# Layer-1 wo products moved into the tail of the forward attention, and shorter chains of small operations, in a two-layer decode kernel with backward pass

## The chip, the cores and the metric

The kernel runs on one core of a Trainium2 chip. The metric is the device time of one execution in microseconds (us); the time before is the median of three runs.

## The reference, cut to what matters

Two layers share one set of weights. Each layer is attention over a KV cache and then an MLP, for two sequences of one token each; the kernel returns the output and the gradients of all inputs.

```python
def _A_ref(x, k_cache, v_cache, wq, wo):     # x (2,1,1024), caches (2,4,16384,128), 32 query heads
    q = heads(x @ wq)                        # wq (1024,4096)
    p = softmax(q @ k.T * 128**-0.5)
    return merge(p @ v) @ wo                 # wo (4096,1024)
def _B_ref(x, w1, b1, w2, b2):               # w1 (1024,3584), w2 (3584,1024)
    return gelu(layernorm(x) @ w1 + b1) @ w2 + b2
x = x + _A_ref(layernorm(x), ...)            # layer 0
x = x + _B_ref(layernorm(x), ...)
x = x + _A_ref(layernorm(x), ...)            # layer 1, same weights
x = x + _B_ref(layernorm(x), ...)
out, vjp = jax.vjp(all of it); return out, vjp(grad_out)
```

`_B_ref` normalizes its input a second time, so the MLP has two norms in a row, which the kernel folds into one (`ln2_fwd`).

## The kernel before

Everything is in one program with a manual schedule: each engine executes its instructions in the order in which the Python code emits them. All loads go through one queue on SyncE (SP in the profile), in program order. Loads of 1 MiB land in a ring of seven buffers (`ld`, `NLD = 7`, tiles named `wt`, `kv_K`, `kv_V`); a load is issued when the buffer's former contents have been used.

The forward attention (`attn_fwd`) walks over eight groups g (sequence, KV head), each in 16 slots of eight 128-column blocks of K: TensorE (PE) transposes a block (`tp`), VectorE (DVE) or ScalarE (ACT) copies it out, PE multiplies with q (`sc`). After the last slot of a group `post` queues the rest on a small scheduler (`Sched`): maxima (`pm`), 16 exponentials on ACT (`e_all`), 64 products with V in eight quads (`Acc.quad`, into one half of the PSUM bank `ACCT`, group g in half g % 2), the evacuation `acc_sb`, a product with `sel2` (`o_ps`) and the scaling `oT`. K of group 7 is kept in SBUF, so that in the last group the load queue has already gone on to `wo`.

After `attn_fwd`, `attn_layer_fwd` casts `oT` into `o_all`, and `w_fwd` clears `ACCT` and multiplies the eight tiles of `wo` (four blocks of 128 rows each; 32 products a tile, line 362). Tile k of `wo` needs heads 4k to 4k + 3, which come from groups k // 2 and 4 + k // 2. The sum is `xA`. Then `mlp_hidden`: `ln2_fwd` (two sums over the partitions by PE, in `part_sum`, with a product by -1/D after the first), products with the seven tiles of `w1` (`w_fwd` with `keep`), and the gelu chain on DVE with one exponential on ACT.

In layer 1 the tiles of `w1` are kept for the backward pass (class `Back`): tiles 0 to 3 are transposed in place by DVE (`turn32`, line 294), tiles 4 to 6 by PE in units of eight transposes (`wtp`, line 395) with copies by ACT (line 159). The last units are emitted after all forward products and before the gelu:

```python
hps = w_fwd(B_w1, D, F, m_all[:, 0:DJ, lsl(l)], keep=keep)
if keep is not None:
    for k in range(len(keep.tiles)):
        keep.some(k, 1 if k == len(keep.tiles) - 1 else 4)
    copies_on(None)
```

`weights_down` then carries the gradient back through `w1` (`Back.banks` clears two PSUM banks, `open` spreads the gradient into small blocks by the products `spg` and the DVE product `Gw` or `blocks`, `run` does the products `dm_d` and `dm_p`, `columns` folds the first into `dm_f`), through the norm (`ln_bwd`, sum `lb_ps`), and through `wo` (eight tiles again, `do_d` and `do_p`). Then `attn_bwd` goes over the caches for layer 1, `attn_in_bwd` and `w2b` go through the norm and `w2`, `weights_down` follows for layer 0, and a last long stage does the attention backward of layer 0 while it writes the gradients of the caches and the weights. The tail ends with the norm's backward pass of layer 0 and the store of the input's gradient.

Of the kernel before, what the change touches and what calls it, by code (L numbers as in the profile page):

```python
# [19 lines left out]
LN_EPS = 1e-5  # L20
# [3 lines left out]
def kernel(  # L24
# [88 lines left out]
    V.memset(onesf[:], 1.0)  # L113
    ones_bf = const.tile([128, 2], BF16, name="ones_bf")
# [72 lines left out]
    def part_sum(src, n, name):  # L187
        ps = pm_([128, n], F32, name)
        PE.matmul(ps[:], lhsT=onesf[:], rhs=src, start=True, stop=True)
        return ps  # L190
# [18 lines left out]
    def ln_fwd(xT, name):  # L209
        s1 = small.tile([128, 2], F32, name="ln_s1")  # L210
        V.tensor_reduce(out=s1[:], in_=xT.rearrange("p j b -> p b j"), axis=AX.X, op=ALU.add)
        ps = part_sum(s1[:], 2, "ln_ps")
        negmu = small.tile([128, 2], F32, name="ln_negmu")
        V.tensor_scalar(out=negmu[:], in0=ps[:], scalar1=-1.0 / D, scalar2=None, op0=ALU.mult)
# [6 lines left out]
        ps2 = part_sum(s2[:], 2, "ln_ps2")  # L221
        vpe = small.tile([128, 2], F32, name="ln_vpe")
        V.tensor_scalar(out=vpe[:], in0=ps2[:], scalar1=1.0 / D, scalar2=LN_EPS, op0=ALU.mult, op1=ALU.add)
# [6 lines left out]
    def ln2_fwd(xT, name, hook=lambda: None):  # L230

        s1 = small.tile([128, 2], F32, name="ln_s1")
        V.tensor_reduce(out=s1[:], in_=xT.rearrange("p j b -> p b j"), axis=AX.X, op=ALU.add)
        ps = part_sum(s1[:], 2, "ln_ps")
        hook()
        negmu = small.tile([128, 2], F32, name="ln_negmu")
        V.tensor_scalar(out=negmu[:], in0=ps[:], scalar1=-1.0 / D, scalar2=None, op0=ALU.mult)
        xc = wrk.tile([128, DJ, 2], F32, name="ln_xc")
        V.tensor_tensor(out=xc[:], in0=xT, in1=bcast_j(negmu[:], DJ), op=ALU.add)
        sq = wrk.tile([128, DJ, 2], F32, name="ln_sq")  # L240
        V.tensor_tensor(out=sq[:], in0=xc[:], in1=xc[:], op=ALU.mult)
        s2 = small.tile([128, 2], F32, name="ln_s2")
        V.tensor_reduce(out=s2[:], in_=sq[:].rearrange("p j b -> p b j"), axis=AX.X, op=ALU.add)
        ps2 = part_sum(s2[:], 2, "ln_ps2")
        vpe = small.tile([128, 2], F32, name="ln_vpe")
        V.tensor_scalar(out=vpe[:], in0=ps2[:], scalar1=(1.0 + LN_EPS) / D, scalar2=LN_EPS * LN_EPS, op0=ALU.mult,
                        op1=ALU.add)
        rstd = vec.tile([128, 2], F32, name=name + "_rstd")
        nc.gpsimd.tensor_tensor(out=rstd[:], in0=vpe[:], in1=neghalf[:], op=ALU.pow)
        y = vec.tile([128, DJ, 2], F32, name=name + "_y")  # L250
        V.tensor_tensor(out=y[:], in0=xc[:], in1=bcast_j(rstd[:], DJ), op=ALU.mult)
        return y, rstd

    def ln_bwd(dy, y, rstd, name, hook=lambda: None, after=lambda: None, twice=False):
        t1 = wrk.tile([128, DJ, 2], F32, name="lb_t1")
        V.scalar_tensor_tensor(out=t1[:], in0=dy, scalar=1.0 + LN_EPS if twice else 1.0, in1=y, op0=ALU.mult,
                               op1=ALU.mult)
        s = small.tile([128, 2, 2], F32, name="lb_s")
        V.tensor_reduce(out=s[:, 0, :], in_=dy.rearrange("p j b -> p b j"), axis=AX.X, op=ALU.add)
        V.tensor_reduce(out=s[:, 1, :], in_=t1[:].rearrange("p j b -> p b j"), axis=AX.X, op=ALU.add)  # L260
        hook()
        ps = part_sum(s[:].rearrange("p a b -> p (a b)"), 4, "lb_ps")
        after()
        nm = small.tile([128, 2, 2], F32, name="lb_nm")
        V.tensor_scalar(out=nm[:].rearrange("p a b -> p (a b)"), in0=ps[:], scalar1=-1.0 / D, scalar2=None,
                        op0=ALU.mult)
        u = wrk.tile([128, DJ, 2], F32, name="lb_u")
        V.tensor_tensor(out=u[:], in0=y, in1=bcast_j(nm[:, 1, :], DJ), op=ALU.mult)
        V.tensor_tensor(out=u[:], in0=u[:], in1=dy, op=ALU.add)
        V.tensor_tensor(out=u[:], in0=u[:], in1=bcast_j(nm[:, 0, :], DJ), op=ALU.add)  # L270
        dx = wrk2.tile([128, DJ, 2], F32, name=name, tag="lb_dx")
        V.tensor_tensor(out=dx[:], in0=u[:], in1=bcast_j(rstd, DJ), op=ALU.mult)
        return dx
# [51 lines left out]
    def columns(acc, fin):  # L325

        n = acc.shape[-1] // 32
        xt = ktp.tile([128, 8, 128], BF16, name="xt", tag="kT")
        x = xt[:].rearrange("p a b -> p (a b)").bitcast(F32)[:, 0:n * 32]
        V.transpose(out=x, in_=acc)  # L330
        xv = x.rearrange("p (n m) -> p n m", m=32)
        for q in range(4):
            PE.matmul(fin[32 * q:32 * q + 32], lhsT=fold[:], rhs=xv[:, :, 2 * q:2 * q + 2], start=True, stop=True,
                      tile_position=(0, 32 * q))
# [31 lines left out]
    def w_fwd(W, n_in, n_out, x, between=None, keep=None):  # L366
        JO = n_out // 128
        nw = min(WIDE, 512 // JO)
        fps = ACCT[:, 0:JO * nw].rearrange("p (j b) -> p j b", b=nw)
        V.memset(fps, 0.0)  # L370
# [27 lines left out]
    class Back:  # L398
# [41 lines left out]

        def banks(self):
            if self.nd:
                self.acc = px([128, 512], F32, self.name + "_d")
                V.memset(self.acc[:, 0:32 * self.nd], 0.0)
            if self.np:
                self.p = px([128, self.np, WIDE], F32, self.name + "_p")
                V.memset(self.p[:], 0.0)

        def open(self, gT):
            self.gT = gT  # L450
            self.G = g_tile(self.n_o, self.n_o == 8)
            self.spread(0)
# [30 lines left out]
        def columns(self):  # L483
            self.d = px([128, self.nd, 2], F32, self.name + "_f")
            columns(self.acc[:, 0:32 * self.nd], self.d)

        def parts(self):
            out = []
# [123 lines left out]
    def attn_fwd(l, q_bf, rbc, oT, groups):  # L612
# [10 lines left out]
        def post(g):  # L623
# [36 lines left out]
            def finish(ps):  # L660
                V.tensor_tensor(out=oT[:, g, :], in0=ps, in1=rbc[:, g, :], op=ALU.mult)
# [30 lines left out]
        while s < len(slots) + 2 or sch.busy():  # L692
# [7 lines left out]
            if 2 <= s < len(slots) + 2:  # L700
                score(s - 2)
            s += 1

    def attn_bwd(l, do_bf, dqT, dn, groups, ahead):
# [30 lines left out]
        def wq_sum():  # L735
            fin = px([128, DJ, 2], F32, "dn_fin")
            columns(both[:, 256:512], fin)
            V.tensor_copy(out=dn[:], in_=fin[:])
# [116 lines left out]

    def attn_layer_fwd(l, xT, between=None):
# [9 lines left out]
        attn_fwd(l, qT_bf, rbc, oT, ALLG)  # L866
        for b in range(2):
            V.tensor_copy(out=o_all[:, 0:HQ, 2 * l + b], in_=oT[:, b * HKV:(b + 1) * HKV, :].rearrange("p k r -> p (k r)"))
        aps = w_fwd(A_wo, HD, D, o_all[:, 0:HQ, lsl(l)])
# [4 lines left out]

    def mlp_hidden(l, xT, keep=None):
        y2, rstd2 = ln2_fwd(xT[:], f"m{l}")
# [3 lines left out]
        hps = w_fwd(B_w1, D, F, m_all[:, 0:DJ, lsl(l)], keep=keep)  # L880
        if keep is not None:
            for k in range(len(keep.tiles)):
                keep.some(k, 1 if k == len(keep.tiles) - 1 else 4)
            copies_on(None)
# [6 lines left out]
        u = wrk.tile([128, FJ, 2], F32, name="g_u")  # L891
        V.tensor_tensor(out=u[:], in0=w_[:], in1=hpre[:], op=ALU.mult)
        z = wrk.tile([128, FJ, 2], F32, name="g_z")
        S.activation(out=z[:], in_=u[:], func=ACT.Exp, scale=2.0 * GELU_C)
        if keep is not None:
            V.tensor_scalar(out=x2[:], in0=x2[:], scalar1=3.0 * GELU_A * GELU_C * 0.5, scalar2=GELU_C * 0.5,
                            op0=ALU.mult, op1=ALU.add)
            V.tensor_tensor(out=x2[:], in0=x2[:], in1=hpre[:], op=ALU.mult)
        V.tensor_scalar(out=z[:], in0=z[:], scalar1=1.0, scalar2=None, op0=ALU.add)
        rz = wrk.tile([128, FJ, 2], F32, name="g_rz")  # L900
        V.reciprocal(out=rz[:], in_=z[:])
        th = vec.tile([128, FJ, 2], F32, name=f"th{l}")
        V.tensor_scalar(out=th[:], in0=rz[:], scalar1=-2.0, scalar2=1.0, op0=ALU.mult, op1=ALU.add)
        hh = wrk.tile([128, FJ, 2], F32, name="g_hh")
        V.tensor_scalar(out=hh[:], in0=th[:], scalar1=1.0, scalar2=0.5, op0=ALU.add, op1=ALU.mult)
        d1 = None
        if keep is not None:
            t2 = wrk.tile([128, FJ, 2], F32, name="gb_t2", tag="g_z")
            V.tensor_tensor(out=t2[:], in0=th[:], in1=th[:], op=ALU.mult)
            V.tensor_scalar(out=t2[:], in0=t2[:], scalar1=-1.0, scalar2=1.0, op0=ALU.mult, op1=ALU.add)  # L910
            V.tensor_tensor(out=x2[:], in0=x2[:], in1=t2[:], op=ALU.mult)
            d1 = vec.tile([128, FJ, 2], F32, name=f"gb_d1{l}")
            V.tensor_tensor(out=d1[:], in0=hh[:], in1=x2[:], op=ALU.add)
# [4 lines left out]
        saved[f"m{l}"] = dict(y2=y2, rstd2=rstd2, hpre=hpre, th=th, xT=xT, w1=keep, d1=d1)  # L918
# [8 lines left out]
    def mlp_slope(l):  # L927
        sv = saved[f"m{l}"]
        hpre, th = sv["hpre"], sv["th"]
        t2 = wrk.tile([128, FJ, 2], F32, name="gb_t2", tag="g_z")  # L930
        V.tensor_tensor(out=t2[:], in0=th[:], in1=th[:], op=ALU.mult)
        V.tensor_scalar(out=t2[:], in0=t2[:], scalar1=-1.0, scalar2=1.0, op0=ALU.mult, op1=ALU.add)
        x2 = wrk.tile([128, FJ, 2], F32, name="gb_x2", tag="g_rz")
# [769 lines left out]
```

## Time and profile before

| | us |
|---|---|
| median of 3 runs | 1118.36 (1116.38 to 1119.42) |
| the profiled execution | 1124.0 |
| its span, first to last instruction | 1122.2 |
| PE, DVE, ACT busy in the span | 919.0, 615.2, 532.3 |
| DMA moved | 441.83 MB, mean 394 GB/s |

Shares of busy time are means over stages of different kinds. The row GB/s of the page cuts the span into 40 slices of 28 us and tells where the transfers are at their usual rate of some 420 GB/s and where they aren't. The chain of waits is followed back from the last instruction; between 395 and 495 us, the stages around the change, it goes mostly through PE and the loads of `w1` and `wo`.

### The profile page before, as it was taken

The page shows a single profiled execution, that of the slowest core. Times are in us where ns is not written, and L with a number is a line of the kernel's source. Part 1 is how long each engine was busy: PE and PEld are TensorE (multiplying, and loading weights), DVE is VectorE, ACT ScalarE, POOL GpSimd, SP SyncE. Part 2 cuts the span into 40 slices and gives each one's busy share as a digit, 9 for nine tenths or more (in the row PEclk, how much of TensorE's full clock was granted, in tenths as well). Part 3 has the DMA queues.
Part 4 walks back from the last instruction along what each step waited for, and adds up shares of the span by engine and source line. Part 5 has one row for each costly group of instructions (what it writes and reads, how often), then busy time and mean ns, then how long its engine had stood idle before and what let it go on. Part 6 is the DMA issues. An engine that isn't in the chain of part 4 may idle for free.

```text
span 1122.2 us, 37948 instructions
## 1 busy us (share of the span) xinstructions
PE 919.0 (82%) x16706; PEld 674.1 (60%) x16707; DVE 615.2 (55%) x1333; ACT 532.3 (47%) x1352; POOL 69.0 (6%) x122
## 2 busy tenths in 40 slices
PE   3979796458889886789987877889898896999996
PEld 3867674357677656678765676655554453455552
DVE  1545442071355434554443357479698775787776
ACT  0535352004545341334433234468587775686765
POOL 0000000000000000000000000022021111111210
PEclk9989786557899876899988899999799897797878
DMA  9999999999999988799999999998999999999997
GB/s 370 423 424 425 423 425 415 395 413 420 423 413 424 423 311 302 287 426 420 387 415 422 392 398 327 376 355 312 405 367 420 424 418 424 405 400 420 422 408 290
DMA packets 99973, 441.83 MB, mean 394 GB/s; under 512 B 7126, under 2 KB 10198, under 8 KB 62688
## 3 DMA queue, kind: packets, MB, share of 16 engines
q1 hardware_dynamic: 82464, 347.12, 76.7%
q0 software_dynamic: 17344, 92.29, 20.0%
q8 instruction: 130, 2.13, 0.7%
q14 instruction: 35, 0.29, 0.1%
HBM read 340.80 MB, written 98.58 MB: 392 GB/s over the span
## 4 chain that ended last, share of the span: by engine, by line
PE 50%; DMA 31%; DVE 11%; ACT 4%; issue 4%; POOL 0%; DVEq 0%; SPq 0%; POOLq 0%; ACTq 0%
DMA kv_V<-in_A_v_cache_dram 10%; PE tp L531 10%; DMA wt<-in_B_w_dram 5%; PE tpm L1610 5%; DMA kv_K<-in_A_k_cache_dram 5%; PE acc_all L563 4%; PE xm L1419 4%; DMA wt<-in_A_wo_dram 4%; PE xm L1333 3%; PE sc L684 3%; PE dp L1472 3%; PE wtp L395 2%; DMA keepK<-in_A_v_cache_dram 2%; PE dp L779 2%; DMA out_dram<-keepK 2%
## 5 line engine op out<-in xcount | busy, mean ns | idle before, releaser
L159 ACT COPY kT<-tp 128x512 int32<-128x512 int32 x201 | 118.0, 587 | 289.3 <-PE tp L531 277.0
L162 DVE COPY kT<-tp 128x1024 bf16<-128x1024 bf16 x167 | 114.2, 691 | 136.5 <-PE tp L531 126.3
L531 PE MATMUL tp<-ident,kv_K 128*128 128x128 bf16 x1728 | 145.3, 233 | 4.0 <-DMA kv_K<-in_A_k_cache_dram 3.7
L531 PEld LDWEIGHTS <-kv_K 128*128 128x128 bf16 x1728 | 110.2, 104 | 4.8 <-DMA kv_K<-in_A_k_cache_dram 4.5
L170 DVE CAST big<-xm 128x512 bf16<-128x512 f32 x133 | 86.4, 685 | 23.7 <-PE xm L1419 13.4
L167 ACT CAST big<-xm 128x512 bf16<-128x512 f32 x151 | 82.1, 595 | 24.9 <-PE xm L1333 13.4
L684 PEld LDWEIGHTS <-kT 128*128 128x128 bf16 x2048 | 76.3, 98 | 27.6 <-issue 22.1
L684 PE MATMUL sc<-qT_bf,kT 128*128 128x8 bf16 x2048 | 91.8, 171 | 0.0
L167 ACT CAST keepV<-xm 128x512 bf16<-128x512 f32 (+1 forms) x137 | 75.1, 594 | 32.2 <-PE xm L1419 20.3
L362 PEld LDWEIGHTS <-wt 128*128 128x128 bf16 x1920 | 57.2, 104 | 54.6 <-DMA wt<-in_B_w_dram 16.6
L159 ACT COPY wt<-wtp 128x512 int32<-128x512 int32 x70 | 39.0, 587 | 89.9 <-PE wtp L395 79.4
L648 ACT ACTIVATE e_all<-sc,negm 128x64 bf16<-128x64 f32 x256 | 77.2, 342 | 1.1 <-DVE negm L643 1.0
L170 DVE CAST keepV<-xm 128x512 bf16<-128x512 f32 (+1 forms) x101 | 66.0, 685 | 21.1 <-PE xm L1419 14.2
L531 PE MATMUL tp<-ident,kv_V 128*128 128x128 bf16 x864 | 70.1, 228 | 5.8 <-DMA kv_V<-in_A_v_cache_dram 4.4
L563 PE MATMUL acc_all<-kv_V,e_all 128*16 128x256 bf16 x864 | 46.6, 296 | 28.9 <-DMA kv_V<-in_A_v_cache_dram 13.8
L294 DVE STREAM_TRANSPOSE wt<-wt 128x512 int32<-128x512 int32 x106 | 64.5, 674 | 7.7 <-PE w2b_f L362 5.6
L531 PEld LDWEIGHTS <-kv_V 128*128 128x128 bf16 x864 | 55.5, 102 | 7.6 <-DMA kv_V<-in_A_v_cache_dram 4.7
L648 ACT ACTIVATION_READ_ACCUMULATOR e_all<-sc,negm 128x1 f32 x256 | 59.4, 232 | 0.0
L167 ACT CAST keepK<-xm 128x512 bf16<-128x512 f32 x98 | 52.8, 595 | 11.5 <-PE xm L1419 7.5
L1472 PE MATMUL dp<-wdo,kT 128*128 128x64 bf16 x896 | 52.7, 206 | 0.0
L1419 PE MATMUL xm<-QmK,blk 64*128 64x512 bf16 x256 | 47.7, 437 | 2.3 <-ACT keepV L167 1.0
L170 DVE CAST keepK<-xm 128x512 bf16<-128x512 f32 x69 | 44.8, 684 | 8.6 <-PE xm L1419 6.6
(380 smaller groups left out, 1557.7 us busy)
## 6 DMA issues: line engine op xcount, KB each, us to landing
kv_K<-in_A_k_cache_dram SPq DMA_DIRECT2D x81, 1024.0 KB, 12.5
kv_V<-in_A_v_cache_dram SPq DMA_DIRECT2D x81, 1024.0 KB, 12.0
wt<-in_B_w_dram SPq DMA_DIRECT2D x35, 1024.0 KB, 12.9
wt<-in_A_wo_dram SPq DMA_DIRECT2D x32, 1024.0 KB, 8.7
out_dram<-big POOLq DMA_DIRECT2D x26, 1024.0 KB, 17.1
out_dram<-keepV POOLq DMA_DIRECT2D x19, 1024.0 KB, 17.5
out_dram<-keepK POOLq DMA_DIRECT2D x17, 1024.0 KB, 16.2
wt<-in_A_wq_dram SPq DMA_DIRECT2D x16, 1024.0 KB, 10.9
```

The costliest lines, as they stand in the source:

```text
L159: S.copy(out=dst.bitcast(I32), in_=src.bitcast(I32))
L162: V.tensor_copy(out=dst, in_=src)
L167: S.copy(out=dst, in_=src)
L170: V.tensor_copy(out=dst, in_=src)
L294: V.transpose(out=w, in_=w)
L362: PE.matmul(fps[:, o0 + o, :].rearrange("p (a b) -> p a b", b=2), lhsT=wv[:, j, o * 128:(o + 1) * 128], rhs=x[:, j0 + j, :].unsqueeze(1).t ...
L531: PE.transpose(tp[:, j, :], cv[:, b * 8 + j, :], ident[:])
L563: PE.matmul(self.acc[cg:cg + 16, :], lhsT=coef(u), rhs=self.cv[:, t:t + 2, :].rearrange("p t d -> p (t d)"), start=False, stop=True, tile_ ...
L648: S.activation(out=e_all[:, g, f * half:(f + 1) * half, l, h, :], in_=sc[g][f][:, h, :].rearrange("p (a b) -> p a b", b=2), func=ACT.Exp, ...
L684: PE.matmul(sc[g][f][:, :, t % TH], lhsT=kT[:, j, :], rhs=q_bf[:, g, :], start=True, stop=True)
L1419: PE.matmul(pss[k][:], lhsT=blk[p:p + 64, o + 2 * h + k // 2, :], rhs=Qm[p:p + 64, :, :].rearrange("p a b -> p (a b)"), start=True, stop=T ...
L1472: PE.matmul(dp[:, :, t:t + 4], lhsT=kT[:, j, :], rhs=wd[:, :, x:x + 4], start=(b + j == 0), stop=False)
```

## The change

1. `attn_fwd` writes `o_all` itself, one more DVE product for each group in `finish`, in place of the two casts at the end, and calls `tail(step)` in the steps after the last slot. In layer 1, `tail` clears half 0 of `ACCT` at step 6, takes the tiles of `wo`, and emits the products of tiles 0 to 5 in steps 6 to 10, amid the last group's work; tiles 6 and 7 follow after `attn_fwd`. At step 9 it takes and clears the PSUM bank for the `w1` products (`h_ps`).
2. The norms: a matrix of -1/D (`onesn`) in the sums makes the products by 1/D go away, and the next operations read the sums from PSUM; `ln_bwd` takes `dy` and its product with y side by side and sums both with one reduction; `ln2_fwd` is merged into `ln_fwd`.
3. The gelu: exp(-2cu) and a reciprocal give the gate `hh` at once; three operations fewer before `h_all`, and four fewer in the slope for the backward pass in layer 1, three fewer in `mlp_slope`.
4. PSUM clears are moved: for `dm_d`, `dm_p` into a hook of `ln_fwd`, for `do_p` behind `lb_ps`, for `do_d` behind the first `blocks`, likewise for `w2b` and for `w1` of layer 0.
5. The leftover PE transposes of `w1` (five units of eight) move from before the gelu into `run`; in layer 1 the fold adds into `dm_p`, so that one copy does instead of a copy and a sum.
6. `open` spreads the first tile that DVE has transposed at once, instead of when its products come up; so `spg` and `blocks` go ahead of other transposes.

```diff
@@ attn_fwd
             def finish(ps):
+                kv = g % HKV
+                V.tensor_tensor(out=o_all[:, kv * 8:(kv + 1) * 8, 2 * l + g // HKV], in0=ps, in1=rbc[:, g, :], op=ALU.mult)
                 V.tensor_tensor(out=oT[:, g, :], in0=ps, in1=rbc[:, g, :], op=ALU.mult)
...
+            if s >= len(slots):
+                tail(s - len(slots))
@@ attn_layer_fwd
-        attn_fwd(l, qT_bf, rbc, oT, ALLG)
-        for b in range(2):
-            V.tensor_copy(out=o_all[:, 0:HQ, 2 * l + b], in_=oT[:, b * HKV:(b + 1) * HKV, :].rearrange("p k r -> p (k r)"))
-        aps = w_fwd(A_wo, HD, D, o_all[:, 0:HQ, lsl(l)])
+        def prod(k):
+            fwd_rows(fps, WIDE, wvs.pop(k), o_all[:, 0:HQ, lsl(l)], tiles[k][0], 0)
+
+        def tail(step):
+            if l == 0:
+                return
+            if step == 6:
+                V.memset(fps, 0.0)
+                for k in range(NLD):
+                    take(k)
+                prod(0)
+                take(NLD)
+            if 6 <= step < 11:
+                prod(step - 5)
+            if step == 9:
+                h_bank[l] = px([128, 512], F32, "h_ps")
+                V.memset(h_bank[l][:, 0:FJ * (512 // FJ)], 0.0)
+
+        attn_fwd(l, qT_bf, rbc, oT, ALLG, tail)
...
+            for k in list(wvs):
+                prod(k)
@@ ln_fwd
-        ps = part_sum(s1[:], 2, "ln_ps")
-        negmu = small.tile([128, 2], F32, name="ln_negmu")
-        V.tensor_scalar(out=negmu[:], in0=ps[:], scalar1=-1.0 / D, scalar2=None, op0=ALU.mult)
+        negmu = part_sum(s1[:], 2, "ln_ps", onesn)
+        hook()
@@ ln_bwd
-        V.tensor_reduce(out=s[:, 0, :], in_=dy.rearrange("p j b -> p b j"), axis=AX.X, op=ALU.add)
-        V.tensor_reduce(out=s[:, 1, :], in_=t1[:].rearrange("p j b -> p b j"), axis=AX.X, op=ALU.add)
+        V.tensor_reduce(out=s[:].rearrange("p (a b) -> p a b", b=2), in_=pair[:].rearrange("p a j b -> p a b j"),
+                        axis=AX.X, op=ALU.add)
         hook()
-        ps = part_sum(s[:].rearrange("p a b -> p (a b)"), 4, "lb_ps")
+        nm = part_sum(s[:], 4, "lb_ps", onesn)
         after()
-        V.tensor_scalar(out=nm[:].rearrange("p a b -> p (a b)"), in0=ps[:], scalar1=-1.0 / D, scalar2=None,
-                        op0=ALU.mult)
@@ mlp_hidden
-        if keep is not None:
-            for k in range(len(keep.tiles)):
-                keep.some(k, 1 if k == len(keep.tiles) - 1 else 4)
-            copies_on(None)
...
-        S.activation(out=z[:], in_=u[:], func=ACT.Exp, scale=2.0 * GELU_C)
+        S.activation(out=z[:], in_=u[:], func=ACT.Exp, scale=-2.0 * GELU_C)
...
-        V.reciprocal(out=rz[:], in_=z[:])
-        V.tensor_scalar(out=th[:], in0=rz[:], scalar1=-2.0, scalar2=1.0, op0=ALU.mult, op1=ALU.add)
-        V.tensor_scalar(out=hh[:], in0=th[:], scalar1=1.0, scalar2=0.5, op0=ALU.add, op1=ALU.mult)
+        V.reciprocal(out=hh[:], in_=z[:])
@@ Back.open
-            self.spread(0)
+            self.spread(next(k for k in range(len(self.tiles)) if self.dve(k) > self.tiles[k][0]))
@@ weights_down
-        wob.banks()
-        dx = ln_bwd(dm[:], sv["y2"][:], sv["rstd2"][:], "dx", lambda: some(2), lambda: some(4), True)
+        dx = ln_bwd(dm, sv["y2"][:], sv["rstd2"][:], "dx", lambda: some(2), lambda: (wob.bank_p(), some(4)), True)
         gn = vec.tile([128, DJ, 2], F32, name=f"gM{l}")
+        V.tensor_tensor(out=gA_all[:, 0:DJ, lsl(l)], in0=dx[:], in1=gT[:], op=ALU.add)
+        wob.open(gA_all[:, 0:DJ, lsl(l)])
+        wob.bank_d()
         V.tensor_tensor(out=gn[:], in0=dx[:], in1=gT[:], op=ALU.add)
-        V.tensor_copy(out=gA_all[:, 0:DJ, lsl(l)], in_=gn[:])
-        wob.open(gA_all[:, 0:DJ, lsl(l)])
         some(8)
```

The number and order of the loads on the SP queue and of the stores on GpSimd's queue stay as they are; on PE the same number of products and transposes is in another order.

## The prediction

> **What bounds the kernel now.** I read the page's slices first, since 441.83 MB at the usual 420 GB/s are 1052 us: for most of the 1122 us the link can't be beaten, and an edit pays only where transfers pause.
>
> ```profile
> span 1122.2 us, 37948 instructions
> ...
> GB/s 370 423 424 425 423 425 415 395 413 420 423 413 424 423 311 302 287 426 420 387 415 422 392 398 327 376 355 312 405 367 420 424 418 424 405 400 420 422 408 290
> ```
>
> Slices 15 to 17 (393 to 477 us) move 311, 302 and 287 GB/s: just where the last group of layer 1's attention, `wo`, `w1` and the gelu lie. So I cut that place by windows (columns: busy time of PE, weight loads, DVE, ACT, POOL; granted clock, DMA share, GB/s):
>
> ```profile
> 400.00:416.00 16.00, 12.06 (x220) 8.09 (x218) 5.11 (x15) 7.75 (x48) 0.00 (x0) 0.76 0.98 356
> 416.00:423.00 7.00, 5.64 (x141) 4.92 (x142) 1.31 (x6) 0.00 (x0) 0.00 (x0) 0.50 0.17 32
> 423.00:444.00 21.00, 12.36 (x358) 11.69 (x355) 11.83 (x26) 1.17 (x2) 1.44 (x4) 0.58 1.03 394
> 444.00:457.00 13.00, 8.22 (x215) 7.52 (x216) 4.61 (x20) 4.05 (x8) 0.00 (x0) 0.76 0.07 19
> 457.00:490.00 33.00, 25.35 (x641) 22.99 (x630) 18.87 (x56) 11.64 (x21) 0.00 (x0) 0.91 1.03 408
> ```
>
> The link stands still twice, 7 us and 13 us, because all seven buffers are full and their products wait: first for the end of the attention, then for the gelu. In between eight tiles take 21 us, 2.6 each. The timeline shows what holds them:
>
> ```profile
> 412.58 1.88 PE L563 MATMUL acc_all<-keepV,e_all 128*16 128x256 bf16 x32 [1.82 <-ACT e_all L648]
> ...
> 419.85 6.16 PE L362 MATMUL acc_all<-o_all,wt 128*128 128x32 bf16 x224 [0.82 <-DVE acc_all L370]
> ...
> 427.27 0.96 PE L362 MATMUL acc_all<-o_all,wt 128*128 128x32 bf16 x32 [1.26 <-DMA wt<-in_A_wo_dram]
> ...
> 445.72 0.99 PE L362 MATMUL acc_all<-m_all,wt 128*128 128x18 bf16 x32
> ...
> 450.25 0.25 ACT L894 ACTIVATE g_z<-g_u 128x56 f32<-128x56 f32 x1
> ...
> 454.86 4.80 SPq L356 DMA_DIRECT2D wt<-in_A_wo_dram  x5
> ```
>
> Seven tiles of `wo` are multiplied in one go from 419.85; the eighth can be issued only at 420.9, after the first (the DMA view: 6.3 us to landing), so PE waits for it until 427.27. The chain of waits goes the same way, and later through the norm's backward pass and DVE's in-place transposes:
>
> ```profile
> 426.39 14.06 DMA wt<-in_B_w_dram
> ...
> 449.77 0.59 ACT wt L159
> ...
> 471.48 7.95 DMA wt<-in_A_wo_dram
> ...
> 693.29 4.86 DVE wt L294 x8
> ```
>
> **The change part by part**, at the profiled execution's times (1124.0, 5.6 above the median, of which 1.8 lie outside the span; I take the gain over to the median unchanged).
>
> *The tail.* `o_ps` of group 6 ends at 410.76. The same product of group 7 ended at 419.02, and `wo` began 0.82 later, with two casts between; I take 0.7, so the products of tiles 0 to 5 may begin at 411.45. 224 took 6.18, 27.6 ns each: five tiles (160) run to 415.85. Their tiles: the seventh was issued at 409.2 and took 8.8 by the DMA view, to 418.0; at 2.6 apart the fifth is there at 412.8 and the sixth at 415.4, needed at 414.97 and 416.3. Cover 0.9; without it PE waits, and the quads of group 7 are queued behind. Those quads pay: before they began at 412.58 and ended at 417.5; now one quad (0.47), tile 5 (0.88), five quads (2.35), the sum and two quads (1.5) end at 421.05. Evacuation to `oT` took 1.7: 422.75. Casts and clear are gone; two tiles take 1.77: 424.5 instead of 428.2. **3.7 earlier**. The seven `o_all` products of the earlier groups (0.17 each) and the clears at step 6 and 9 lie on a DVE that is busy half the time; uncovered they cost 1.2 and 0.75.
>
> *Norm and clear.* From `xA` to the first `w1` product it took 4.52. `ln_negmu` goes (0.19), but two clears of 0.27 stand before `ln_xc` and keep 0.1 of it; the clear of 504 columns (0.48 and its handover) leaves the path. `w1` may start at 428.5 instead of 432.79.
>
> *The link.* The eighth tile is issued behind tile 0's products, at 412.4, while the link is still busy, and five tiles of `w1` follow to 417.2. So there is no pause: eight tiles after 418.0 at 2.6 land until 438.8. The last two are issued at 423.7 and 424.6, 12 us ahead. Before, the last was awaited at 445.72. **6.9 earlier**, and PE and DVE keep up: 16 transposes of 0.60 on DVE from 428.9 end at 438.5. `hpre` moves from 446.74 to 439.85.
>
> *Gelu.* From `hpre` to `spg` it took 6.13: the exponential stood behind ACT's copies of the five leftover units until 450.25, 2.5 later than its input. Now it can start at +1.0; with 0.25, then 0.23, 0.54 (reciprocal), three products of 0.25 and the handover `spg` comes at +2.85. **3.3 more**; and 0.1 since `Gw` no longer stands behind two clears. The products begin 10.3 earlier, at 443.5, and the first reload of `wo` likewise, at 444.55 instead of 454.86.
>
> *The bill.* The five units now stand in `run`. It took 9.0 (453.79 to 462.81). New order: two tiles 1.9, `Gw` 0.7, one tile 0.95, 16 transposes, a tile 0.95, 16 transposes, a tile 0.97, 32 transposes, two tiles 1.76. Sixteen transposes took 1.87 at 441.37 with clock 0.50 and 1.05 at 446.56 with 1.00; I take the first 16 at the slow and the rest at the fast: 12.4. Of 10.3, **6.9 stay** at `dm_f`. In the norm's backward pass the sum, the scaling and two clears (1.87 from `dm_f` to `lb_ps`) leave 1.1, which PE's 16 transposes set: +0.75. Then `spg` (0.27) stands ahead of the products: the eighth `wo` tile is issued at 464.1 (was 471.48). Its predecessor lands 10.3 earlier; a single load took 5.8 to 6.3, so it lands at 470.1, **9.3 earlier**. DVE starts its 16 transposes only behind `blocks`, at 462.8, and ends at 472.5 (was 479.46); the last products, from there, end at 475.4 (`do_f` was 484.33), 8.9 earlier. `mlp_slope` drops three operations (0.6) ahead of the first copies of `attn_bwd`. I put the stage at **9.4**: compute gains 9.5 and the loads 9.3.
>
> *The second pass through `w2`, `w1`, `wo` (640 to 709 us).* The clears leave the way of `lb_ps` (0.8), but PE then waits for `dh_all` before `spg` (0.75 lost), and no longer waits for `Gw` at 675 (0.83 won); `o_row`, behind DVE's transposes, comes 1.1 earlier. Before the next `lb_ps` 0.96 of clears go, of which 0.75 count. `blocks` no longer waits behind eight transposes (the 4.86 of the chain), but these now wait for `blocks`; products at 696.45 instead of 698.51, end 706.6 instead of 708.6. **2.0** (0 to 3.5; the chain has pauses of 0.8 to 2.0 named "issue" that any order can hit).
>
> *The end.* In the last `ln_bwd` the first reduction ran beside the product, so merging saves nothing; `lb_nm` saves **0.2**. Layer 0's norms, gelu and casts: the link is full there (share 1.0 until 400 us); nothing, and 1.5 won if that cover were gone.
>
> Sum 9.4 + 2.0 + 0.2 = **11.6**: profile 1112.4, median **1106.8**.
>
> [...] Reading sums from PSUM: `xA` (from PSUM) and `ln_xc` (from SBUF) both took 0.17, so I charge nothing. [...] The clock: the rows show 0.50 from 430 to 446 and 1.00 after PE had been dense. [...]
>
> **Rivals.** *Half clock through `w1` and `wo`:* 48 transposes in `run` and 64 in the `wo` part that ran at 1.00 each pay 0.82 per sixteen: 5.7; gain 5.9, 1112.5. For it: 0.58 mean from 423 to 444. Against: 0.91 from 457 on, with PE no denser than it will be.
> *The gain is taken back:* `attn_bwd` follows, and the link is full there; if a buffer that frees late sets its end, the lead is lost: 1118. Against: loads and products both move by over 9, and the chain crosses that stage in turn through both.
> *Slower:* layer 1's `attn_bwd` runs at clock 1.00 from 490 to 560 with PE busy 9.3 to 10 of 10. Loads that lead by 9 us change where PE pauses; eight transposes take 0.61 at full and 1.01 at half clock (490.42). With more than 29 of its some 140 slots newly at half clock the 11.6 are gone; with 60 it is 1131. Against: the same instructions in the same order follow, and pauses there come from the loads, which get earlier.
>
> **How the numbers follow.** The forecast's mechanism with gains of 8 to 16: 0.62; half clock or another loss that leaves 3.5 to 8: 0.22; a larger gain 0.03; taken back 0.05; slower 0.08. The likeliest sum is 11.6, so 1106.8. Low end: second pass 3.5, no slow transposes (0.8) and 2.0 of "issue" pauses avoided, 1102.5. High end: the half-clock rival with 2.0 of further pauses, 1114.5. Outside lie the 0.13 of the last two and some 0.05 at the low end and the bad edge of the second. Faster by over 0.3% (3.4 us, about what a measurement of this kernel tells from no change) 0.87, within 0.05, slower 0.08.
>
> **What would show it.** In the profile after: `wo` products of 160 at about 411.4, without a wait for DMA; the first pause of the link gone and the second shorter, some 9 us; `xA` near 424.5; the last `w1` product near 439; the exponential 1.0 behind `hpre`; the first `wo` reload near 444.5; `do_f` near 475. I'm wrong if PE waits for `wo` in the tail, if the link pauses after 464, if the leftover transposes take 1.87 per sixteen throughout, or if `attn_bwd` ends less than 8 us earlier than 641.5, where the first `w2` product stood.

## The result and the profile after

The changed kernel takes **1106.18 us** (median of 4 runs, 1105.8 to 1107.5) against 1118.89 (1116.38 to 1119.85): ratio 0.9884, 95% interval 0.9855 to 0.9913. The forecast was 1106.8 within 1102.5 to 1114.5. The profiled execution took 1106.4 with a span of 1104.3; that of before took 1124.0, so the two traces differ by 17.6 where the medians differ by 12.7. From the last fold of the second pass (`do_f` of layer 0) to the end, the profiled execution of before needs 413.7 us; in the thirteen other executions profiled below this stretch takes between 403.8 and 411.8. What the traces differ by in the last stage is therefore not put down to the change.

The page's slices, whole span:

```profile
span 1104.3 us, 37946 instructions
...
GB/s 370 423 425 424 424 425 416 397 412 423 425 409 418 424 390 329 328 424 420 405 413 420 383 386 340 397 356 330 412 407 423 423 418 425 422 416 418 424 377 305
```

Slices 15 to 17 move 390, 329 and 328 GB/s instead of 311, 302 and 287. The windows of the changed kernel (columns as before: PE, weight loads, DVE, ACT, POOL, granted clock, DMA share, GB/s):

```profile
400.00:416.00 16.00, 12.90 (x305) 10.26 (x302) 5.90 (x17) 7.49 (x46) 0.00 (x0) 0.79 1.00 367
416.00:438.00 22.00, 16.63 (x407) 14.65 (x407) 10.90 (x28) 1.17 (x2) 1.42 (x4) 0.63 1.00 380
438.00:447.00 9.00, 5.02 (x171) 4.61 (x170) 5.20 (x18) 1.42 (x3) 0.00 (x0) 0.69 0.14 41
447.00:480.00 33.00, 27.75 (x664) 25.09 (x665) 17.80 (x50) 14.16 (x26) 0.00 (x0) 0.92 1.03 400
```

The first pause of the link (7 us at 416) is gone: the DMA share is 1.00 from 400 to 438. The second is 9 us long instead of 13. The timeline shows what stands around it:

```profile
411.30 3.90 PE L341 MATMUL acc_all<-o_all,wt 128*128 128x32 bf16 x141 [0.65 <-DVE acc_all L876]
...
413.19 14.26 SPq L335 DMA_DIRECT2D wt<-in_B_w_dram  x7
...
417.30 0.63 PE L341 MATMUL acc_all<-o_all,wt 128*128 128x32 bf16 x19 [2.10 <-issue]
...
440.74 0.25 ACT L930 ACTIVATE g_z<-g_w 128x56 f32<-128x56 f32 x1 [1.18 <-DVE g_w L928]
...
444.46 17.47 SPq L335 DMA_DIRECT2D wt<-in_A_wo_dram  x8
```

The `w1` loads are issued from 413.2 on (in before from 421.7), the exponential starts 0.98 behind `hpre` (439.76; DVE's first operation behind the last `w1` product), and the first reload of `wo` stands at 444.46 instead of 454.86. PE waits for no load in the tail, but pauses 2.1 us for "issue" after 141 products. The chain of waits goes into `hpre` through DVE's in-place transposes, and later through the eighth `wo` tile:

```profile
433.24 6.60 DVE wt L273 x11
439.83 0.15 DVE hpre L922
...
461.56 8.14 DMA wt<-in_A_wo_dram
```

### The profile page after: what moved, and what is told of

Its sections match the earlier page's. It is cut to its first block, busy times and chain, and to the rows that moved or that the text cites. A ratio compares the mean times of both kernels' runs of the same rounds, so it can differ in the third digit from the quotient of the medians.

```text
span 1104.3 us, 37946 instructions
## 1 busy us (share of the span) xinstructions
PE 908.3 (82%) x16706; PEld 670.6 (61%) x16707; DVE 612.4 (55%) x1324; ACT 531.0 (48%) x1352; POOL 68.7 (6%) x122
## 4 chain that ended last, share of the span: by engine, by line
PE 51%; DMA 29%; DVE 12%; issue 4%; ACT 3%; POOL 0%; SPq 0%; DVEq 0%; POOLq 0%; ACTq 0%
PE tp L520 11%; DMA kv_V<-in_A_v_cache_dram 9%; DMA kv_K<-in_A_k_cache_dram 5%; PE acc_all L552 5%; PE tpm L1629 5%; PE xm L1438 4%; DMA wt<-in_B_w_dram 4%; DMA wt<-in_A_wo_dram 4%; PE sc L675 3%; PE xm L1352 3%; PE wtp L375 3%; PE dp L1491 3%; DMA out_dram<-keepxV 2%; DMA keepK<-in_A_v_cache_dram 2%; PE dp L772 2%
## 5 line engine op out<-in xcount | busy, mean ns | idle before, releaser
L552 PE MATMUL acc_all<-kv_V,e_all 128*16 128x256 bf16 x864 | 47.0, 298 | 26.2 <-DVE acc_all L535 12.7
L375 PE MATMUL wtp<-ident,wt 128*128 128x128 bf16 x560 | 45.4, 240 | 4.8 <-ACT wt L161 2.4
## 6 DMA issues: line engine op xcount, KB each, us to landing
kv_K<-in_A_k_cache_dram SPq DMA_DIRECT2D x81, 1024.0 KB, 12.7
```

What stands on the lines that cost most here:

```text
L375: PE.transpose(tp[:, o, :], view[:, o * 128:(o + 1) * 128], ident[:])
L552: PE.matmul(self.acc[cg:cg + 16, :], lhsT=coef(u), rhs=self.cv[:, t:t + 2, :].rearrange("p t d -> p (t d)"), start=False, stop=True, tile_ ...
```

## The experiments

The times of e1 to e12 were each measured beside those of the kernel before, on the same chip. The table gives, from one trace of each kernel, `hpre` of layer 1, the issue of the first reload of `wo`, the time from there to the landing of its last bytes, `do_f` of layer 1 (the fold that ends the stage), and the stretch from the first `w2` product of the second pass to `do_f` of layer 0; then the median and the ratio to before with its 95% interval.

| kernel | hpre | first reload | to last landing | do_f 1 | second pass | median | ratio, 95% |
|---|---|---|---|---|---|---|---|
| before | 446.74 | 454.86 | 24.6 | 484.02 | 67.0 | 1118.9 | 1 |
| after | 439.76 | 444.46 | 25.2 | 474.46 | 67.3 | 1106.18 | 0.9884 (0.9855-0.9913) |
| e1 tail only | 440.68 | 449.39 | 24.6 | 478.46 | 67.7 | 1113.44 | 0.9951 (0.9934-0.9968) |
| e2 leftovers only | 446.55 | 452.13 | 24.5 | 482.54 | 68.3 | 1117.55 | 0.9987 (0.9968-1.0006) |
| e3 no tail | 446.47 | 451.17 | 25.1 | 481.39 | 67.4 | 1112.89 | 0.9948 (0.9929-0.9967) |
| e4 leftovers back | 439.73 | 446.94 | 24.8 | 476.78 | 66.8 | 1108.04 | 0.9905 (0.9881-0.9928) |
| e5 chains only | 446.64 | 453.86 | 25.3 | 484.21 | 65.9 | 1115.54 | 0.9966 (0.9949-0.9982) |
| e6 late spread | 440.80 | 445.50 | 25.1 | 475.12 | 66.5 | 1108.07 | 0.9905 (0.9882-0.9928) |
| e7 early products | 440.53 | 445.19 | 25.3 | 475.55 | 68.4 | 1108.4 | 0.9903 (0.9881-0.9926) |
| e8 PE tile first | 440.20 | 444.09 | 25.3 | 474.17 | 70.8 | 1106.27 | 0.9889 (0.9861-0.9916) |
| e9 prefetch | 440.58 | 445.28 | 23.2 | 474.85 | 65.5 | 1107.07 | 0.9895 (0.9869-0.9922) |
| e10 all three | 441.09 | 445.00 | 22.6 | 475.87 | 66.3 | 1105.87 | 0.9886 (0.9860-0.9912) |
| e11 after again | 440.22 | 444.92 | 25.3 | 474.93 | 68.0 | 1105.23 | 0.9897 (0.9864-0.9929) |
| e12 64 shifted | 441.76 | 446.46 | 24.5 | 475.15 | 68.7 | 1109.04 | 0.9915 (0.9884-0.9946) |

**e1, the tail alone**, in the kernel before:

```diff
-        attn_fwd(l, qT_bf, rbc, oT, ALLG)
-        (two casts into o_all)
-        aps = w_fwd(A_wo, HD, D, o_all[:, 0:HQ, lsl(l)])
+        attn_fwd(l, qT_bf, rbc, oT, ALLG, tail)   # finish writes o_all; tail as in the change, without h_bank
```

> The kernel before with the tail alone: o_all written group by group, wo products of tiles 0 to 5 of layer 1 amid the last group's work. Link theory (the gain is the two pauses of the load queue; the eighth wo tile and the w1 tiles are issued from about 412 us): last w1 product near 439.5 instead of 446.7, hpre, dm_d, the first reload of wo and do_f of layer 1 each 6.5 to 7 us earlier, the time 6.5 us (5 to 7.5) below before, about 1112.4. Chain theory (the shorter chains of small operations carry the gain, and a pause removed at 416 us only comes back at 438 us): hpre less than 3 us earlier and the time 0 to 3 below before.

`hpre` came 6.1 earlier, the first reload and `do_f` 5.5, the time 0.49% (5.5 us, 3.6 to 7.4). The marks fall short of the link theory's 6.5 to 7 by up to 1 us, but they are about twice the chain theory's 3, and the time lies in the link theory's range: it holds in the main. The pause at 416 doesn't come back at 438: the window 438 to 452 holds one pause of the old length (26 GB/s), and no other is there.

**e2, the leftovers alone**, in the kernel before:

```diff
         hps = w_fwd(B_w1, D, F, m_all[:, 0:DJ, lsl(l)], keep=keep)
-        if keep is not None:
-            for k in range(len(keep.tiles)):
-                keep.some(k, 1 if k == len(keep.tiles) - 1 else 4)
-            copies_on(None)
```

> The kernel before with one edit: the five leftover units of PE transposes of w1 are taken out of the gelu and fall into run. Bill theory: the exponential starts some 2.5 us earlier, dm_d and the first reload of wo likewise 2.5 to 3.3 earlier, but run grows from 9.0 to about 12.4 us, so dm_f, lb_ps and the issue of the eighth wo tile stand where they stood (within 1 us): time the same as before, within 1.0 us, about 1118.9. Rival (the move is worth what it frees, since the loads lead by it): 2.5 to 3.3 us below before, about 1116.

The first reload came 2.7 earlier, `lb_ps` stood within 0.02 us of where it was: the bill is real. But the last bytes of `wo` landed 2.8 earlier and `do_f` came 1.5 earlier, and the time, 0.13% less with an interval that holds no change, can't tell the two theories apart.

**e3, no tail**, in the changed kernel:

```diff
         def tail(step):
             if l == 0:
                 return
-            if step == 6: ...        # clear, takes, product 0
-            if 6 <= step < 11:
-                prod(step - 5)
             if step == 9: ...
         attn_fwd(l, qT_bf, rbc, oT, ALLG, tail)
-        if l == 0: ...               # clear, takes, all products; else the products left over
+        V.memset(fps, 0.0)
+        for k in range(len(tiles)):
+            take(k)
+            prod(k)
```

> The changed kernel with the tail taken out: all eight wo tiles of layer 1 are taken and multiplied behind the attention, ACCT cleared there; the clear of the w1 bank stays at step 9. Link theory: the pause of the load queue at 416 us is back, last w1 product 6 to 7 us later, the time 6.5 us (5.5 to 8) above the changed kernel, about 1112.7. Chain theory: at most 2 us above it, about 1107.5.

1112.89, 6.7 above the changed kernel; `hpre`, the first reload and `do_f` are 6.7 to 6.9 later. The pause is back, in the windows of this kernel:

```profile
416.00:423.00 7.00, 5.81 (x143) 4.95 (x140) 1.14 (x5) 0.00 (x0) 0.00 (x0) 0.50 0.13 44
...
444.00:453.00 9.00, 5.02 (x160) 4.70 (x161) 3.45 (x14) 1.42 (x3) 0.00 (x0) 0.69 0.09 21
```

**e4, the leftovers back** before the gelu, in the changed kernel:

```diff
         hps = w_fwd(B_w1, D, F, m_all[:, 0:DJ, lsl(l)], keep=keep, bank=h_bank.get(l))
+        if keep is not None:
+            for k in range(len(keep.tiles)):
+                keep.some(k, 1 if k == len(keep.tiles) - 1 else 4)
+            copies_on(None)
```

> The changed kernel with the five leftover units of w1 put back between the w1 products and the gelu. Bill theory: the exponential starts 2 to 2.7 us later, dm_d and the first reload 2.5 to 3.3 later, run 3.4 shorter, lb_ps and do_f within 1 us of the changed kernel: time within 1.0 us of it, about 1106.2. Rival (the earlier loads pay): 2.5 to 3.3 us above it, about 1109.

This run corrected my theory. `lb_ps` stands within 0.1 us of the changed kernel, as the bill says, and the eighth `wo` tile is issued at the same time (461.46 against 461.56). Yet it lands 2.0 later, and `do_f` is 2.3 later. Timeline and chain of this kernel:

```profile
443.24 0.25 ACT L934 ACTIVATE g_z<-g_w 128x56 f32<-128x56 f32 x1
446.94 14.88 SPq L335 DMA_DIRECT2D wt<-in_A_wo_dram  x8
```

```profile
461.46 10.26 DMA wt<-in_A_wo_dram
```

The exponential, 2.5 later, makes the first reload 2.5 later, and the eighth load waits 10.26 instead of 8.14 us: it stands in a queue. From here on the theory was: *the eight tiles land one after another, and the last bytes come some 25 us after the first reload, whenever the eighth is issued.* The column of the table says so for the twelve executions that load eight tiles: 24.5 to 25.3, over 10.8 us of difference in the first reload, and with the eighth issued 14.5 to 18.8 us behind the first. e9 and e10 test it by taking bytes out. In time e4 is 1.9 above the changed kernel, with intervals that overlap.

**e5, the chains only**: e3 and e4 together.

> The changed kernel without the tail and with the five leftover units of w1 back before the gelu: only the shorter norms, gelu, sums, the moved clears and the early spread are left of the change. Queue theory (the stage of layer 1 ends 24.5 to 25.2 us after the first reload of wo is issued, plus some 5): first reload 1.0 to 1.3 us earlier than before, do_f of layer 1 likewise, the second pass 0.5 earlier, time 1.5 to 2.5 us below before, about 1117. Sum of the differences so far (12.7 less 6.1 for the tail less 1.7 for the leftovers): 4.9 us below before, about 1114. Prediction's terms for these parts (gelu 0.8, norm 0.75, second pass 2.0, end 0.2): about 3.7 below, 1115.

The first reload came 1.0 earlier, `do_f` of layer 1 not at all (0.2 later), the second pass 1.1 shorter. So the queue theory's forecast for `do_f` (1.0 to 1.3 earlier) missed. The time is 0.34% less, 3.8 us (2.0 to 5.7; 2.8 between the medians). The marks account for about 1 of it, the second pass; the ratio lies nearest to the prediction's terms (3.7). Where the rest of it lies isn't settled.

**e6, late spread**, one line of `open`:

```diff
-            self.spread(next(k for k in range(len(self.tiles)) if self.dve(k) > self.tiles[k][0]))
+            self.spread(0)
```

> The changed kernel with one edit: open spreads tile 0 only, so blocks for wo are formed when the third tile's products come up, behind DVE's transposes. Prediction's step (blocks ahead of the transposes was worth most of the 2.0 us of the second pass): do_f of layer 0 1.5 to 2 us later against the first w2 product, time 1.5 to 2 us above the changed kernel, about 1108. Theory that DVE's transposes now wait for blocks instead, so that one wait took the place of the other: do_f of layer 0 within 0.7 us, time within 1.0 us, about 1106.2.

The second pass took 66.5 us, not longer than with the early spread (67.3, 68.0). The time, 1108.07, is 1.9 above the changed kernel, which is what the prediction's step forecast, but the intervals overlap and can't decide. The chain of e6 goes through eight transposes and then `blocks`:

```profile
680.58 4.71 DVE wt L273 x8
685.29 0.32 DVE blocks L285
```

That of the changed kernel goes through `blocks`, a clear, and then four transposes:

```profile
684.08 0.04 DVE blocks L285
...
684.61 0.48 DVE do_d L423
...
685.16 2.36 DVE wt L273 x4
```

From the start of `gA_all` to the first `do_d` product it is 5.8 us in the changed kernel, 5.2 in its second profile (e11), 5.9 in e6 and 5.3 in the kernel before. By these marks one wait took the place of the other.

**e7, early products** of the first `wo` tile, directly behind `spg`:

```diff
-        some(8)
-        wob.run()
+        some(2)
+        wob.prod(0)
+        wob.run(first=1)      # run leaves out the product of tile 0
```

with `some(2)` for `some(4)` in `ln_bwd`'s second hook.

> The changed kernel with the products of the first turned wo tile put directly behind spg, ahead of the second tile's transposes, in both layers. Queue theory (the eighth wo tile lands 24.5 to 25.2 us after the first reload whatever its own issue): the eighth tile is issued 1 to 2 us earlier (about 460) and lands at 469.7 as before it, do_f of layer 1 within 0.5 us, time within 1.0 us of the changed kernel. Issue theory of the prediction (its own issue sets its landing): lands 1 to 2 us earlier, do_f likewise, time about 1104.7.

Counted from the first reload, the eighth tile was issued 1.1 earlier (16.0 against 17.1 us) and landed 25.3 after it. Nothing was gained; the time, 1108.4, is 2.2 above the changed kernel, with intervals that overlap.

**e8, a tile for PE first**: its transposes amid the forward products, its products ahead of `spg`.

```diff
-        return Back(B_w1, D, F, 4, range(7), "dm", by_tile=[True, True, True, True, False, False, False])
+        return Back(B_w1, D, F, 4, [4, 0, 1, 2, 3, 5, 6], "dm", by_tile=[False, True, True, True, True, False, False])
...
-            w1b.open(dh_all[:, 0:FJ, lsl(l)])
+            w1b.gT = dh_all[:, 0:FJ, lsl(l)]
+            w1b.prod(0)
+            w1b.open(w1b.gT)
```

> The changed kernel with the tiles of w1 in layer 1 taken in another order: a tile that PE transposes comes first, its transposes are made amid the w1 products, and its products stand ahead of spg, so they wait for dh_all alone; two DVE units fall into run. Queue theory: the first reload of wo is issued 0.7 to 1.0 us earlier (443.5 to 443.8), the eighth lands at about 468.9, do_f of layer 1 at 473.9, time 0.8 us below the changed kernel, about 1105.4. Issue theory: the eighth tile's issue and lb_ps stand where they stood, so do_f within 0.3 us of 474.7 and the time the same, 1106.2.

Counted from `hpre`, the first reload came 0.8 earlier (3.9 against 4.7 us) and the last bytes 25.3 behind it; but `hpre` itself was 0.4 later, so that 0.3 was left at `do_f` and nothing in time.

**e9, prefetch**: three of the eighth tile's four row blocks go into idle kT buffers, behind the last `w1` load.

```diff
+            for u in range(3):
+                t = ktp.tile([128, 8, 128], BF16, name="woq%d" % u, tag="kT")
+                wo_pre.append(t[:].rearrange("p a b -> p (a b)"))
+                nc.sync.dma_start(wo_pre[u], A_wo[(28 + u) * 128:(29 + u) * 128, :])
...                          # the fourth row block follows the seven reloads
```

> The changed kernel with one addition: three of the four row blocks of the eighth wo tile of layer 1's backward pass are loaded behind the last w1 tile into three kT buffers that stand idle there, in the pause of the link before the first reload; only the fourth row block (0.25 MiB) is left in the queue behind the seven reloads. Queue theory: first reload at 444.5 as in the changed kernel, the last wo bytes land 1.9 us earlier, about 467.8 (23.2 us after the first reload instead of 25.2), do_f of layer 1 1.5 to 1.9 us earlier, about 473.0, time 1.5 us below the changed kernel, about 1104.7. Rival (products and DVE's transposes set the end of the stage): the bytes land earlier and do_f stays within 0.5 us of 474.7, time the same.

The queue shortened as it should: 23.2 instead of 25.2. But `do_f` stood at 474.85, not 473.0 (counted from the first reload 0.4 earlier, not 1.5 to 1.9): here the rival's forecast came true. Now DVE's transposes and the products set the end, in this timeline:

```profile
461.80 9.60 DVE L273 STREAM_TRANSPOSE wt<-wt 128x512 int32<-128x512 int32 x16
...
472.63 0.72 DVE L309 STREAM_TRANSPOSE xt<-do_d 128x512 f32<-128x512 f32 x1 [1.24 <-PE do_d L300]
...
474.16 0.56 PE L463 MATMUL do_p<-gA_all,woq 128*128 128x32 bf16 x16 [1.28 <-issue]
```

DVE's 16 transposes end at 471.4, and PE pauses 1.28 for "issue". So the queue theory tells when the bytes land, and no longer when the stage ends: in the changed kernel the last bytes landed at 469.70 and the same 16 transposes ended at 470.24, 0.5 us apart.

**e10**, e7 to e9 together:

> The three edits together: three row blocks of the eighth wo tile loaded ahead, a PE-transposed tile of w1 first with its products ahead of spg, the first wo tile's products directly behind spg. Queue theory: first reload 444.1, last wo bytes at 467.4, do_f of layer 1 1.8 to 2.5 us earlier than in the changed kernel, about 472.5, time about 1104. Rival (products and transposes set the end): do_f within 0.7 us of 474.7, time 1106 to 1107.

Last bytes 22.6 after the first reload, first reload 445.0, `do_f` 475.87: later than either theory allowed (472.5; 474.7 within 0.7), because `hpre` came 1.3 later. Counted from `hpre` it is 34.8 us, against 34.7 in the changed kernel: the shorter queue gained nothing. No version beat the changed kernel by more than the intervals.

**e11**, the changed kernel once more:

> The changed kernel once more, for more executions to compare with. Every theory: median within 1.5 us of 1106.2, first reload of wo at 444.5 (0.3 each way), its eighth tile landing 24.5 to 25.5 us later, do_f of layer 1 at 474.7 (0.7 each way). Against the slow profiled execution of the kernel before: the stages from 720 to 850 us as fast as in the other kernels, end near 1104.5.

1105.23; all ten executions of this kernel have a median of 1106.0. First reload 444.92, 0.1 later than the range expected, and `do_f` 474.93 as expected. A query gradient of the last stage (`dqT`) is written at 824.60, where the profile of before had 843.32: 18.7 earlier, of which 10.1 were there at `do_f` of layer 0; the rest arose in the last stage, and is not put down to the change.

**e12, 64 instructions ahead.** PE's pauses for "issue" had come at the same places of the program each time: e11's chain has 1.99 us at 414.53 (again after 141 products), 2.22 at 649.07 and 1.53 at 692.55; that of the changed kernel:

```profile
415.20 2.10 issue
...
649.54 2.21 issue
...
693.64 1.48 issue
```

```diff
+    pad = pt([128, 8, 128], BF16, "pad")
+    for o in range(32):
+        PE.transpose(pad[:, o % 8, :], ident[:], ident[:])
```

> The changed kernel with 32 transposes of the identity (64 PE instructions, 32 of them weight loads) added at the very start, their result unused; everything behind them stands 64 places later in PE's stream of instructions. In seven runs with the tail, PE paused 2.0 to 2.3 us for nothing but issue behind the 141st to 143rd wo product, and in the trace an instruction packet of 16 KiB moved at that moment, the next 5.9 us later. Supply theory (PE waits for the next block of its instructions, and blocks end at fixed places of the stream): the pause moves 32 products forward, behind product 109 or so, near 414.3, and shrinks or stays (0.5 to 2.2 us); the pause in the w2 products at 649.5 moves likewise. Place theory (something in that work itself, such as buffers or PSUM, stops PE): the pause stays behind product 141. Time under both within 1.5 us of the changed kernel, since the last w1 tile lands at 438.5 either way.

The changed kernel's timeline in the second pass, with pauses after the 18th of 32 `w2b_d` products:

```profile
644.67 0.45 PE L300 MATMUL w2b_d<-wt,blocks 128*8 128x128 bf16 x18
645.81 0.40 PE L300 MATMUL w2b_d<-wt,blocks 128*8 128x128 bf16 x14 [0.68 <-issue]
646.14 0.96 PE L341 MATMUL w2b_f<-h_all,wt 128*128 128x32 bf16 x32
646.95 0.96 PE L453 MATMUL w2b_p<-gM_all,wt 128*128 128x32 bf16 x32
647.76 0.95 PE L341 MATMUL w2b_f<-h_all,wt 128*128 128x32 bf16 x32
649.09 0.45 PE L300 MATMUL w2b_d<-wt,blocks 128*8 128x128 bf16 x18 [0.38 <-DVE wt L273]
651.75 0.59 PE L300 MATMUL w2b_d<-wt,blocks 128*8 128x128 bf16 x14 [2.21 <-issue]
```

e12 (line numbers are 3 higher):

```profile
410.86 4.43 PE L344 MATMUL acc_all<-o_all,wt 128*128 128x32 bf16 x160 [0.65 <-DVE acc_all L879]
...
648.87 0.60 PE L344 MATMUL w2b_f<-h_all,wt 128*128 128x32 bf16 x18
651.93 0.56 PE L344 MATMUL w2b_f<-h_all,wt 128*128 128x32 bf16 x14 [2.45 <-issue]
652.41 0.81 PE L303 MATMUL w2b_d<-wt,blocks 128*8 128x128 bf16 x24
```

In the second pass the pause moved exactly 32 products forward, to behind the 18th product of the group ahead. In the tail it is gone: the 160 products run in one go, and 0.69 is left later, at 418.18. So the supply theory holds, and the place theory falls; that the tail's pause would vanish and not just move was not expected. `xA` came 2.5 earlier than in the changed kernel, and the stage gained nothing by it: in e12 the last `w1` tile decides `hpre`, and it landed at 440.66, 2.2 later than in the changed kernel. Why it was later isn't settled. The time, 1109.04, is 2.9 above the changed kernel, more than the 1.5 that both theories allowed, with intervals that overlap; what the pause costs in time is not shown.

## Why the prediction was right, point by point

- *The tail, 3.7 earlier:* 2.6 (`xA` at 425.70). The products began at 411.30 and waited for no load, as worked out; the 2.1 us pause for "issue" was not in the sum. Without it (e12) `xA` stood at 423.24, better than the 424.5 forecast. By an estimate the error cost 0.3 us at most, since the last `w1` tile landed at 438.46 and its product takes 1.0.
- *Norm and clear, 0.5:* from `xA` to the first `w1` product it took 4.12 instead of 4.52; 4.0 was forecast.
- *The link, 6.9:* `hpre` came 7.0 earlier. The pause at 416 is gone; with the tail taken out (e3) it is back. This step carries about half the gain: 5.5 us on the kernel before (e1), 6.7 on the rest of the change (e3). But "PE and DVE keep up" held without the room that the sum gave it: the last tile landed at 438.46, its product ended at 439.73, behind PE's transposes, and DVE's 16 transposes at 439.84 instead of 438.5, so that in this profile DVE sets `hpre`. In e11 and e12 it is the load, which the chain shows landing at 439.18 and 440.66, just ahead of PE's last `w1` product.
- *Gelu, 3.3:* `dm_d` went from 453.79 to 443.39, 10.4 earlier, 10.3 forecast. e2 and e4 show that moving the leftovers gives 2.5 to 2.7 of it, at the first reload.
- *The bill, 3.4:* too large. `lb_ps` came 9.2 earlier, not 7.65; from the first `dm_d` to the fold it took 11.65 after 8.95, so the bill was 2.7, and from the fold to `lb_ps` 1.5 went where 0.75 was forecast. Only the first 16 leftover transposes were slow (1.82 at a granted clock of 0.50, from 446.90 to 448.70; then 1.00 at 1.00, from 449.40 on), as forecast.
- *Sums read from PSUM:* they cost nothing that the rows show, as charged: `lb_u` takes 0.17 from the sum in PSUM (457.02) and 0.17 from SBUF (457.23).
- *The eighth tile:* it landed 9.7 earlier (9.3 forecast), but the way to that number was wrong. I gave it its own issue and 6.0 us for a single load; in truth it was issued at 461.56, not 464.1, and took 8.14 in a queue whose start is the first reload. The two errors, 2.5 us too late and 2.1 too short, nearly cancel: that the number fits is luck. And it is why the bill is free: what `run` loses is not on the path that ends the stage. e4 shows it (same `lb_ps`, `do_f` 2.3 later).
- *The stage, 9.4:* 9.6 at `do_f` of layer 1.
- *The second pass, 2.0:* the mis-sized term. It took 67.3 us after 67.0. The three executions with the old second pass (before, e1, e2) average 67.7, the eight with the new one as it is (after, e3, e4, e5, e8, e9, e11, e12) 67.5, from 65.5 to 70.8: no gain that can be told from the spread. The step that failed is "`blocks` no longer waits behind eight transposes": e6 undoes it, and its second pass is no longer. Also, four groups of eight transposes that took 0.61 each in before ran at 1.01 (652.50), and sixteen at 678.72 took 1.89 instead of 1.07: the granted clock was 0.50 from 652.50 to 656.60 and from 678.70 to 680.60, where I had not put it, and 1.00 at the same work in before (653.3 to 655.8, 663.2 to 665.7, 689.7 to 690.7).
- *The rivals:* half clock through `w1` and `wo` did not come (clock 0.95 from 457 to 490); `attn_bwd` ran at 1.00 from 490 to 560, and the first `w2` product came at 631.00 instead of 641.52, so neither the slower case nor the gain taken back. (The kernel before was not at 1.00 throughout, as the prediction has it, but at 0.83 from 490 to 500.)
- *The sum:* 9.4 + 2.0 + 0.2 = 11.6 against 12.7 in medians. In the two traces the lead is 9.6 at `do_f` of layer 1, 10.5 at the first `w2` product and 10.2 at `do_f` of layer 0. So the second pass was too high by about its whole 2.0, and some 2.5 of the 12.7 lie in the last stage, where 0.2 was forecast and where the traces differ by up to 10 us among themselves. They are not placed; that the median came within 0.6 of the forecast is to that extent luck. By the ratios of the table the parts add up as 3.8 for the chains (e5), 2.0 more with the leftovers moved (e3 against e5), 7.2 more with the tail (after against e3), each with 2 to 4 us of uncertainty.

## What to carry to other kernels

When loads wait for buffers, look for the first load that can be issued after a pause, and cost an edit by how much earlier that one goes: the last of eight loads landed 24.5 to 25.3 us after it, with its own issue anywhere from 14.5 to 18.8 us behind. An operation of 2.5 us that delayed the first release cost 2.3 at the end of the stage (e4); behind the release it cost nothing there while the queue was the later one. Shortening the queue further gained nothing (e9), because compute ended within 1 us of it. And where one wait is taken from behind another engine's work, work out which of the two orders ends first, since here the two orders ended within 0.7 us of each other, either way round (e6).

## What the runs showed of the hardware

PE stops for its own instructions: with 64 more of them at the start, its pause in the second pass came 32 products earlier in the program (e12). The page of the changed kernel has a queue for them (packets, MB, share):

```profile
q8 instruction: 130, 2.13, 0.7%
```

That is 16 KiB a packet, and PE's 33,413 matmuls and weight loads on 130 packets are 257 a packet. In the trace a packet starts at 415.04, where PE's pause begins at 415.20, and one at 649.50, with the pause at 649.54. The two pauses at 645 and 649 in the second pass are 14 + 32 + 32 + 32 + 18 = 128 products apart, with their weight loads 256 instructions. The records of all fourteen traces bear this out beyond e12. PE has 148 pauses of over 0.4 us for "issue" in them (0.4 to 3.2 us; nine in the changed kernel, 10.5 us together). Counted over PE's records, each of them stands 193 or 194 instructions behind a multiple of 256 (193 at all ten of before and all nine of the changed kernel), and 147 of them end 2.2 to 2.5 us after the start of the last packet.

In these stretches, with the link full (DMA share 1.00 from 400 to 438, 1.05 from 640 to 650), the next packet comes 5.9 us later (415.04, 420.98, 426.92; 643.55, 649.50); 256 instructions of the tail take PE 3.5 us, at 27.7 ns for a product and its weight load (141 products in 3.90). So, by an estimate from these numbers, a dense stretch of small products is held there to about 256 instructions per 5.9 us, and it depends on where the 256 end whether the wait falls into a pause that is there anyway (e12) or into the work. That the loads make the packets late is argued, not tested by an edit. For it: where the DMA share between two packets was 0.95 or more, 27 of 1655 distances were under 5.7 us; where it was 0.5 to 0.8, 12 of 38 were, down to 3.3. Where the pause came at the two places above, it took 1.99 to 2.45 us.
